# Second product's result in columns of 512 and 256, with w_out's conversion and the gate's weights placed later

## The chip, the core and the metric

One NeuronCore of a Trainium2 chip runs the whole program. The metric is the device time of one execution in microseconds (us). Engines are named as in the profile: PE (TensorE matmul), PEld (its weight loads), DVE (VectorE), ACT (ScalarE), POOL (GpSimd), SP (SyncE, whose queue issues most DMAs).

## What is computed

Three layers in a row. First an attention over 4 batches, 12 heads, 448 tokens, head size 64, with an RMS norm of q and k. Its output, 1792 tokens by 768, goes through a dense layer with ELU, and then through a mixture of 8 experts with a greedy assignment of tokens: every expert takes at most 224 tokens, in the order of all logits.

```python
scores = 1/8 * norm(q) @ norm(k).T ; attn = softmax(scores) ; x = attn @ v
h = x @ w_in                      # 768 -> 2048
x = elu(h) @ w_out                # 2048 -> 768      "the second product"
logits = x @ w_gate               # 768 -> 8; sorted, assigned greedily, 224 tokens an expert
out[tokens of e] = relu(x[tokens of e] @ w1[e]) @ w2[e]     # 768 -> 1024 -> 768
```

## The kernel before, in words

Every float32 matrix is split into two float16 parts (high and low), and a product is made of three float16 products (`THREE`, line 496), so a tile costs three matmuls.

The kernel first goes through 24 **pairs of heads** (6 a batch), 16 slots of a written schedule each (lines 737 to 757). A pair is scores (`ps`), softmax on DVE, ACT and POOL (`pe`, `sm`), transposes of the weights (`pta`, `ptb`) and the values (`po`); line 578 on ACT evicts a pair's values, once a pair, and so marks its end. Side work is spread over these slots by the table `spreads` (lines 728 to 733): w_in's conversion from float64 (`w_in_steps`), the hidden layer of the batch before (`hidden`: `ph`, then ELU in `elu_e`, `elu_g`, `gt`), **w_out's conversion** and its product with the gate's weights (`gate_products`, in slots 180 to 280), and the logits of batches 0 and 1 (`late_logits`, slots 295 to 400, `pl`). The logits are taken from the hidden layer directly, with Wg = w_out @ w_gate, which `gate_product` (line 619) makes in 16 pieces f, `pw` on PE and `wgt`/`Wg` on ACT and DVE.

One piece of w_out costs two DMA loads, six DVE instructions (lines 374, 377, 378, at 512 and 256 columns), ACT's lines 380 and 381, POOL's line 382, a store to DRAM and two DMA transposes on SP's queue. `load_gate` (line 597) loads and splits w_gate; `at(-30, load_gate)` puts it before the first scores.

The slots give the order of the program text; a scheduler then orders each engine's instructions, and each engine runs its own list strictly in order.

After the pairs come the hidden layer of the last batch, and the **second product** (`second`, line 804): for each of 14 blocks of 128 tokens, two column halves of DH = 384, 48 matmuls each (`py`), evicted by ACT and DVE to `xh` and stored to DRAM in `x2_d[0]` or `x2_d[1]`. For the last two batches all first halves are made before all second halves (lines 834 to 837). The routing (`Route`) runs in its gaps. Then each expert gathers its tokens' rows from `x2_d[0]` and `x2_d[1]` by POOL's indirect DMAs (`gather`, `xg`), PE transposes them (`pte`), ACT and DVE copy them to `xTe`. Expert 0 first does all products over the first half's KH = 3 chunks of 128 columns, then those of the second half; its inner tiles are `phe` and `phy`, the experts' outputs `pye`. Expert 0's weights are loaded during the routing.

```python
    spreads = [
        ...
        Spread(gate_products(), NG, 180, 280),
        Spread(chain_gens(late_logits(b) for b in range(LB)), 2 * LB * NF // LG, 295, 400),
    ]
    at(-47, load_gain)
    at(-30, load_gate)
```

Of the kernel before, what the change touches and what calls it, by code (L numbers as in the profile page):

```python
# [8 lines left out]
F16 = mybir.dt.float16  # L9
# [246 lines left out]
def kernel(  # L256
# [14 lines left out]
    nc = tc.nc  # L271
    PE, ACT, DVE, POOL = nc.tensor, nc.scalar, nc.vector, nc.gpsimd

    B, H, S, D = q.shape
# [7 lines left out]
    KC = DM // P  # L282
    NF = FF // P
    NF1 = F1 // P
    DH = DM // 2
    NJ = 3
    MAIN = NJ * P
    TAIL = S - MAIN
# [47 lines left out]
    g_d = [dram.tile([P, NF, 2, MAIN], F16, name=f"g_d{b}") for b in range(B)]  # L336

    gt_d = [dram.tile([P, NF, 2, 2 * TAIL], F16, name=f"gt_d{b}") for b in range(B // 2)]
    x2_d = [dram.tile([NCH * P, DM], F16, name=f"x2_d{i}") for i in range(2)]
    wo_d = dram.tile([P, NF, 2, DM], F16, name="wo_d")  # L340

    wuA = ctx.enter_context(tc.tile_pool(name="wuA", bufs=2))
# [254 lines left out]
    def load_gate():  # L597
        nc.sync.dma_start(wg32, w_gate.rearrange("(c p) e -> p c e", p=P))
        ACT.activation(wg16[:, :, 0:NE], wg32, AF.Copy, scale=-SW)
        DVE.scalar_tensor_tensor(wg16[:, :, NE:], wg32, -SW, wg16[:, :, 0:NE], op0=ALU.mult, op1=ALU.subtract)  # L600

    def gate_products():
        wts = None
        for f in range(NF):
            wo = gat.tile([P, 2, DM], F16, name="wo")
            yield from load_steps(wo[:, 0, :], wo[:, 1, :], w_out[f * P:(f + 1) * P, :])
            if f:
                gate_product(f - 1, wts)
                yield
            nc.sync.dma_start(wo_d[:, f], wo)  # L610
            wts = []
            for z in range(2):
                wts.append(gat.tile([P, KC, P], F16, name="wt", bufs=3))
                nc.sync.dma_start_transpose(wts[z], wo[:, z, :])
            yield
        gate_product(NF - 1, wts)
        yield

    def gate_product(f, wts):
# [14 lines left out]

    def logits(pool, tag, b, gs):

        pl = pool.tile([P, S], F32, tag=tag, name="pl")
        kk = key()
        for i, (g, f) in enumerate(gs):
            for z, (o, n) in enumerate(((0, WG), (WG, NE))):  # L640
                mm(pl[o:o + n], Wg[:, f, o:o + n], g[:, z, :], key=kk,
                   start=(i == 0), stop=(i == len(gs) - 1), skip_group_check=True)
        n = WG + NE
        for o, w, c in ((b * MAIN, MAIN, 0), (B * MAIN + b * TAIL, TAIL, MAIN)):
            a = acc[:, o:o + w]
            if gs[0][1] == 0:
                DVE.tensor_copy(a, pl[0:n, c:c + w])
            else:
                DVE.tensor_add(a, a, pl[0:n, c:c + w])

    LB = 2

    def late_logits(b):
        for f in range(0, NF, LG):
            gs = []
            for i in range(f, f + LG):
                gl = gat.tile([P, 2, S], F16, bufs=LG, name="gl")
                nc.sync.dma_start(gl[:, :, 0:MAIN], g_d[b][:, i])
                nc.sync.dma_start(gl[:, :, MAIN:S], gt_d[b // 2][:, i, :, b % 2 * TAIL:(b % 2 + 1) * TAIL])
                gs.append((gl, i))  # L660
            yield
            logits(psT, "pt", b, gs)
            yield

    def hidden(b, xT):

# [57 lines left out]
    def at(t, f, *a):  # L724
# [3 lines left out]
    spreads = [  # L728
        Spread(w_in_steps(0), KC, 40, 96),
        Spread(chain_gens(w_in_steps(i) for i in range(1, FF // WB)), KC * (FF // WB - 1), 96, 176),  # L730
        Spread(gate_products(), NG, 180, 280),
        Spread(chain_gens(late_logits(b) for b in range(LB)), 2 * LB * NF // LG, 295, 400),
    ]
    at(-47, load_gain)
    at(-30, load_gate)
    NSTEP = B * SEQ
    for b in range(B):
        xT = big.tile([P, KC, 2, S], F16, name="xT")
# [56 lines left out]

    gtp = []
    load_g(0)
    xo = rs_.enter_context(tc.tile_pool(name="xo", bufs=3))
    yp = [(psS, "ps")]

    def mmo(*x, **kw):
# [1 line left out]

    def second(rows, g, cols, i):

        o, n = i * DH, DH
        xh = xo.tile([P, 2, DH], F16, name="xh")
        py = yp[-1][0].tile([P, n], F32, tag=yp[-1][1], name="py")
        for f in range(NF):
            u, fu = divmod(f, NF // NU)  # L810
            for (a, z) in THREE:
                mmo(py, g_sb[g][:, f, z, cols], w_out_u[u][:, fu, a, o:o + n],
                    start=(f == 0 and a == 0 and z == 0), stop=(f == NF - 1 and z == 1))
                yield 0.165
        ACT.activation(xh[:, 0], py, AF.Copy, scale=-SX2 / (SG * SW))  # L815
        DVE.scalar_tensor_tensor(xh[:, 1], py, -SX2 / (SG * SW), xh[:, 0], op0=ALU.mult, op1=ALU.subtract)
        nc.sync.dma_start(x2_d[i][rows * P:(rows + 1) * P, :], xh.rearrange("p z d -> p (z d)"))
        yield 0.0
# [68 lines left out]
    rs_.close()  # L887
    psP.append(ctx.enter_context(tc.tile_pool(name="psP0", bufs=1, space=PSUM)))
    ex = ctx.enter_context(tc.tile_pool(name="ex", bufs=2))
    KH = KC // 2  # L890

    def pace_first(e, c):

# [14 lines left out]

    def gather(e):

        xT = [exg.tile([P, 2, KH, CAP], F16, name=f"xTe{i}") for i in range(2)]
        for i in range(2):
            for hh in range(2):
                xg = exg.tile([HD, 2, DH], F16, name="xg", bufs=4)
                POOL.indirect_dma_start(
                    out=xg.rearrange("p z d -> p (z d)"), out_offset=None, in_=x2_d[i],
                    in_offset=bass.IndirectOffsetOnAxis(ap=idx[:, 0, 2 * e + hh:2 * e + hh + 1], axis=0))
                pt = psX.tile([P, 2, KH, HD], F16, tag="pt", name="pte")
                for z in range(2):
                    for c in range(KH):  # L920
                        tr16(pt[:, z, c, :], xg[:, z, c * P:(c + 1) * P], HD)
                (DVE.tensor_copy if hh else ACT.copy)(xT[i][:, :, :, hh * HD:(hh + 1) * HD], pt)  # L922
        return xT
# [91 lines left out]
```

## Time and profile before

| | |
|---|---|
| median of 3 runs | 1150.81 us (1146.79 to 1153.8) |
| the profiled execution's own time | 1149.89 us |
| its span, first to last instruction | 1148.2 us |
| mean granted clock of PE | 0.968 |
| pairs of heads | to about 540 us |
| last hidden layer | about 540 to 620 us |
| second product and routing | about 620 to 883 us |
| experts | about 883 us to the end |

A page's or an answer's row gives busy time of an engine, mean duration of one instruction in ns, and the idle time before it with what ended it. "PEclk" is the share of full clock that PE was granted. Busy PE is not PE at its peak, since matmuls overlap: the distance from start to start tells what one costs.

### The profile page before, as it was taken

Reading aid. Unit: us, or ns where it says so; the run is one execution under the profiler, and the core shown is the slowest. Engines: PE = TensorE matmul, PEld = TensorE weight load, DVE = VectorE, ACT = ScalarE, POOL = GpSimd, SP = SyncE. Lnnn points to the kernel's source line nnn. Section 1 sums busy time; section 2 is a strip of 40 time slices with the busy share of each in tenths; the row PEclk is TensorE's granted clock in tenths of the full one; section 3 lists DMA queues with packets and bytes.
Section 4 is the critical chain, followed back from the end, with each engine's and each line's share of the span. In section 5 each row is a group of like instructions: output and inputs, shape, how many; then the busy total and the mean of one; then the engine's idle time right before and its main releaser. Section 6 shows DMA issues by size and latency. Waiting matters only on the chain.

```text
span 1148.2 us, 19348 instructions
## 1 busy us (share of the span) xinstructions
PE 1037.0 (90%) x7030; PEld 608.9 (53%) x7030; DVE 787.0 (69%) x1567; ACT 538.5 (47%) x1099; POOL 354.1 (31%) x462
## 2 busy tenths in 40 slices
PE   0687879897989989999999999999999799999997
PEld 0233434443544444444444545555546688888885
DVE  3798898999988775654334778887786556666620
ACT  2676677776867765554441111011112455555510
POOL 3677686657756542221001000000000412222100
PEclk9977889999999999999999999999999899999999
DMA  6355575559998736334922151131133778777710
GB/s 173 80 123 130 136 206 164 152 162 246 259 246 207 193 74 135 97 80 148 398 78 69 59 196 59 49 132 49 49 104 100 238 244 247 255 252 255 239 41 25
DMA packets 190319, 176.48 MB, mean 154 GB/s; under 512 B 114704, under 2 KB 161808, under 8 KB 189456
## 3 DMA queue, kind: packets, MB, share of 16 engines
q1 hardware_dynamic: 186064, 163.78, 49.7%
q0 software_dynamic: 3328, 11.01, 3.0%
q8 instruction: 55, 0.90, 0.3%
q10 hardware_dynamic: 832, 0.46, 0.1%
q14 instruction: 40, 0.33, 0.1%
HBM read 125.92 MB, written 31.98 MB: 138 GB/s over the span
## 4 chain that ended last, share of the span: by engine, by line
PE 51%; DVE 18%; DMA 11%; issue 10%; ACT 5%; POOL 3%; SPq 2%; POOLq 0%; DVEq 0%; ACTq 0%
PE py L324 18%; PE ph L324 11%; DMA st<-in_moe_w_dram 4%; PE pye L324 4%; PE po L324 4%; PE phe L324 3%; DVE sm L533 2%; PE ps L324 2%; PE rt_pc L324 2%; DVE cv L377 2%; PE pta L324 2%; DMA qn<-in_q_dram 2%; PE pl L324 1%; DVE cv L378 1%; DVE rt_C L127 1%
## 5 line engine op out<-in xcount | busy, mean ns | idle before, releaser
L324 PE MATMUL ph<-xT,w_in 128*128 128x448 f16 x1152 | 247.2, 359 | 7.8 <-DVE elu_g L685 4.8
L324 PE MATMUL py<-w_out,g 128*128 128x384 f16 x1152 | 203.8, 328 | 0.0
L324 PEld LDWEIGHTS <-w_in 128*128 128x128 f16 x1152 | 108.0, 99 | 125.4 <-issue 44.7
L545 POOL TENSOR_SCALAR pe<-pe,sm 128x448 f32<-128x448 f32 x168 | 127.0, 766 | 141.0 <-DVE sm L541 78.9
L351 DVE SCALAR_TENSOR_TENSOR w<-st,w 128x768 f16<-128x768 f32 (+1 forms) x112 | 119.4, 1073 | 72.1 <-ACT w L350 65.8
L324 PEld LDWEIGHTS <-g 128*128 128x128 f16 x1152 | 107.3, 98 | 81.4 <-issue 18.5
L350 ACT ACTIVATE w<-st 128x768 f16<-128x768 f32 (+1 forms) x112 | 103.8, 933 | 89.3 <-DMA st<-in_moe_w_dram 84.0
L324 PE MATMUL ps<-kT,qT 64*128 64x448 f16 (+1 forms) x576 | 94.3, 382 | 54.5 <-ACT pe L535 29.2
L535 ACT ACTIVATE pe<-ps,sm 128x448 f32<-128x448 f32 x168 | 105.7, 633 | 50.1 <-DVE sm L533 47.6
L324 PE MATMUL pye<-w,hT 128*112 128x512 f16 (+1 forms) x768 | 126.4, 326 | 0.0
L127 DVE TENSOR_SCALAR rt_C<-rt_row,rt_m 128x1792 f16<-128x1792 f32 x98 | 107.3, 1149 | 8.2 <-PE rt_pc L324 7.4
L533 DVE TENSOR_REDUCE sm<-ps 128x1 f32<-128x448 f32 x168 | 100.2, 614 | 17.8 <-PE ps L324 15.5
L324 PEld LDWEIGHTS <-w 128*128 128x128 f16 x1152 | 110.4, 99 | 3.3 <-DVE xTe L922 1.2
L324 PE MATMUL phe<-xTe,w 128*128 128x224 f16 x1080 | 109.2, 261 | 2.1 <-DVE xTe L922 1.1
L324 PEld LDWEIGHTS <-hT 128*112 128x112 f16 x768 | 91.6, 130 | 32.1
L815 ACT ACTIVATE xh<-py 128x384 f16<-128x384 f32 x28 | 13.7, 490 | 176.6 <-PE py L324 159.2
L324 PEld LDWEIGHTS <-qT 64*128 64x128 f16 (+1 forms) x576 | 27.5, 100 | 99.0 <-issue 65.9
L324 PE MATMUL pta<-id,pe 128*128 128x128 f32 x384 | 65.3, 293 | 12.7 <-POOL pe L545 4.7
L685 DVE SCALAR_TENSOR_TENSOR elu_g<-ph,elu_e 128x448 f32<-128x448 f32 x64 | 39.6, 618 | 48.0 <-ACT elu_e L683 47.7
L972 POOL DMA_INDIRECT out_dram<-yo,idx x16 | 18.5, 1155 | 173.9 <-DVE yo L971 172.3
L324 PEld LDWEIGHTS pta<-id,pe 128*128 128x128 f32 x384 | 46.1, 148 | 43.1 <-POOL pe L545 16.0
L201 POOL MEMSET rt_c<- 128x8 f16 x8 | 0.9, 123 | 210.1 <-DVE rt_c L207 206.0
(176 smaller groups left out, 1475.1 us busy)
## 6 DMA issues: line engine op xcount, KB each, us to landing
st<-in_moe_w_dram SPq DMA_DIRECT2D x48, 512.0 KB
st<-in_moe_w_dram SPq DMA_DIRECT2D x64, 384.0 KB
st<-in_moe_w_in_dram SPq DMA_DIRECT2D x24, 512.0 KB
g_d<-gt SPq DMA_DIRECT2D x64, 192.0 KB
g<-g_d SPq DMA_DIRECT2D x16, 768.0 KB
st<-in_moe_w_out_dram SPq DMA_DIRECT2D x16, 512.0 KB
gl<-g_d SPq DMA_DIRECT2D x32, 192.0 KB
wo_d<-wo SPq DMA_DIRECT2D x16, 384.0 KB
```

The source lines that it names most:

```text
L127: i = DVE.tensor_scalar(C.rearrange("p c t -> p (c t)"), row, m[:, s:s + 1], None, op0=ALU.is_le)
L324: i = PE_mm(o, l, r, **kw)
L350: ACT.activation(hi, st, AF.Copy, scale=SW)
L351: DVE.scalar_tensor_tensor(lo, st, SW, hi, op0=ALU.mult, op1=ALU.subtract)
L377: DVE.scalar_tensor_tensor(cv, st[:, :, 1], -0x40000000, cv, op0=ALU.bitwise_and, op1=ALU.bitwise_or)
L378: DVE.scalar_tensor_tensor(cv, st[:, :, 0], 29, cv, op0=ALU.logical_shift_right, op1=ALU.bitwise_or)
L533: i = DVE.tensor_reduce(out=st[:, 0, u:u + 1], in_=ps[u], axis=AX.X, op=ALU.max, negate=True)
L535: ACT.activation(p[:, u, :], ps[u], AF.Exp, bias=st[:, 0, u:u + 1], accum_out=st[:, 1, u:u + 1])
L545: POOL.tensor_scalar(p[:, u, :], p[:, u, :], st[:, 2, u:u + 1], 1.0, op0=ALU.mult, op1=ALU.mult)
L685: DVE.scalar_tensor_tensor(gf, ph, -SG / SH, e, op0=ALU.mult, op1=ALU.min)
L815: ACT.activation(xh[:, 0], py, AF.Copy, scale=-SX2 / (SG * SW))
L972: st = POOL.indirect_dma_start(out=out, out_offset=bass.IndirectOffsetOnAxis(ap=idx[:, 1, 2 * e + hh:2 * e + hh + 1], axis=0), in_=yo, in_ ...
```

## The change

1. The second product's columns are divided 512 and 256 (`PARTS`) instead of 384 and 384, and with them `x2_d`, `xh`, `xg` and `xTe`; expert 0's first round has KH = 4 of 6 chunks. `xg` has two tags with two buffers each, `xh` two buffers instead of three.
2. `gate_products` moves from slots 180 to 280 to slots 240 to 368; `late_logits` goes over f first, then over the batches, in slots 285 to 400.
3. `load_gate` moves from slot -30 to slot 100 of the program text.

```diff
-    DH = DM // 2
+    PARTS = ((0, 512), (512, DM - 512))
...
-    x2_d = [dram.tile([NCH * P, DM], F16, name=f"x2_d{i}") for i in range(2)]
+    x2_d = [dram.tile([NCH * P, 2 * n], F16, name=f"x2_d{i}") for i, (_, n) in enumerate(PARTS)]
...
-    def late_logits(b):
+    def late_logits():
         for f in range(0, NF, LG):
-            gs = []
-            for i in range(f, f + LG):
...
+            for b in range(LB):
+                gs = []
+                for i in range(f, f + LG):
...
-        Spread(gate_products(), NG, 180, 280),
-        Spread(chain_gens(late_logits(b) for b in range(LB)), 2 * LB * NF // LG, 295, 400),
+        Spread(gate_products(), NG, 240, 368),
+        Spread(late_logits(), 2 * LB * NF // LG, 285, 400),
     ]
     at(-47, load_gain)
-    at(-30, load_gate)
+    at(100, load_gate)
...
-    xo = rs_.enter_context(tc.tile_pool(name="xo", bufs=3))
+    xo = rs_.enter_context(tc.tile_pool(name="xo", bufs=2))
...
-        o, n = i * DH, DH
-        xh = xo.tile([P, 2, DH], F16, name="xh")
+        o, n = PARTS[i]
+        xh = xo.tile([P, 2, n], F16, name="xh")
...
-                yield 0.165
+                yield 0.165 * n / 384
...
-    KH = KC // 2
+    KH = PARTS[0][1] // P
...
-        xT = [exg.tile([P, 2, KH, CAP], F16, name=f"xTe{i}") for i in range(2)]
+        xT = [exg.tile([P, 2, n // P, CAP], F16, name=f"xTe{i}") for i, (_, n) in enumerate(PARTS)]
         for i in range(2):
             for hh in range(2):
-                xg = exg.tile([HD, 2, DH], F16, name="xg", bufs=4)
+                n = PARTS[i][1]
+                xg = exg.tile([HD, 2, n], F16, tag=f"xg{i}", name="xg", bufs=2)
```

**Where the instructions go.** Counted in PE's list between the ends of pairs (the 14 `po` matmuls of one pair to those of the next):

| intervals between pairs' ends | before | changed |
|---|---|---|
| 11th to 15th (four) | `pw` 108, `ph` 215 | `pw` 0, `ph` 180 |
| 15th to 23rd (eight) | `pw` 84 (first three), `ph` 348, `pl` 72 | `pw` 192 (24 each), `ph` 414, `pl` 72 |
| 23rd to 24th (one) | `pw` 0, `ph` 46, `pl` 8 | `pw` 0, `ph` 30, `pl` 8 |
| after the last pair | `ph` 273 | `ph` 258 |

DVE's list, right behind the end of the 12th pair, before:

```order
L579 SCALAR_TENSOR_TENSOR xT<-po,xT 128x448
L560 COPY PT<-ptb 128x3x128
L378 SCALAR_TENSOR_TENSOR cv<-st,cv 128x256
L628 TENSOR_TENSOR wgt<-wgt,pw 128x8
L374 TENSOR_SCALAR cv<-st 128x256
L377 SCALAR_TENSOR_TENSOR cv<-st,cv 128x512
L540 TENSOR_SCALAR sm<-sm 128x2
L533 TENSOR_REDUCE sm<-ps 128x1 x2
L629 CAST Wg<-wgt 128x8
L630 CAST Wg<-wgt 128x8
```

and in the changed kernel at the same place (its lines are some six higher):

```order
L580 SCALAR_TENSOR_TENSOR xT<-po,xT 128x448
L561 COPY PT<-ptb 128x3x128
L534 TENSOR_REDUCE sm<-ps 128x1 x2
L561 COPY PT<-ptb 128x3x128
L541 TENSOR_SCALAR sm<-sm 128x2
L542 RECIPROCAL sm<-sm 128x2
L534 TENSOR_REDUCE sm<-ps 128x1 x2
L691 SCALAR_TENSOR_TENSOR elu_g<-ph,elu_e 128x448
```

The softmax's reductions (`sm<-ps`) stand there without w_out's steps (`cv`, `wgt`, `Wg`) ahead of them. Those now stand in the late pairs; DVE's list of the changed kernel behind the end of the 20th pair, where before has none of them:

```order
L580 SCALAR_TENSOR_TENSOR xT<-po,xT 128x448
L561 COPY PT<-ptb 128x3x128
L534 TENSOR_REDUCE sm<-ps 128x1
L375 TENSOR_SCALAR cv<-st 128x512
L378 SCALAR_TENSOR_TENSOR cv<-st,cv 128x512
L541 TENSOR_SCALAR sm<-sm 128x1
L379 SCALAR_TENSOR_TENSOR cv<-st,cv 128x512
L542 RECIPROCAL sm<-sm 128x1
L691 SCALAR_TENSOR_TENSOR elu_g<-ph,elu_e 128x448
```

A reduction that stood directly behind the matmuls' results now has up to two conversions in front of it.

POOL's list at the first gathers, before (x_d_82 is `x2_d[0]`, x_d_83 is `x2_d[1]`; a row is two gathers, one for each half of an expert's tokens):

```order
L915 DMA xg<-x_d_82,idx 112x768 x2
L915 DMA xg<-x_d_83,idx 112x768 x2
L915 DMA xg<-x_d_82,idx 112x768 x2
L915 DMA xg<-x_d_83,idx 112x768 x2
L915 DMA xg<-x_d_82,idx 112x768 x2
```

and in the changed kernel:

```order
L922 DMA xg<-x_d_82,idx 112x1024 x4
L922 DMA xg<-x_d_83,idx 112x512 x4
L922 DMA xg<-x_d_82,idx 112x1024 x2
L922 DMA xg<-x_d_83,idx 112x512 x2
L922 DMA xg<-x_d_82,idx 112x1024 x2
```

Expert 1's rows of the first part are now fetched before expert 0's rows of the second. On PE, before runs the 72 products of expert 0's first round, then 18 `pte` (12 of expert 0's second part, 6 of expert 1), then the second round. The changed kernel runs 70 of its 96, four `pte` of the second part, two more products, four `pte`, the other 24, 16 `pte` of expert 1, then the second round of 48. The gate's weights come earlier than their new slot: on DVE line 600's instruction stands behind the last of the first pair's preparation, before the first reduction of scores, where it stood ahead of the second sum of squares.

## Rows read from the trace of the kernel before

**Rows 1.** The page: the span.
```profile
span 1148.2 us, 19348 instructions
```

**Rows 2.** Windows: length; busy PE, PEld, DVE, ACT, POOL (count); PEclk, DMA share, GB/s.
```profile
252.00:354.00 102.00, 89.08 (x577) 44.13 (x574) 96.33 (x223) 74.25 (x183) 68.36 (x80) 0.95 0.99 251
...
411.00:517.00 106.00, 102.31 (x626) 49.26 (x623) 66.39 (x161) 61.90 (x149) 30.69 (x46) 1.00 0.40 93
```

**Rows 3.** Line 578, the pairs' ends: 11th to 17th, then 18th to 24th.
```profile
L578 ACT ACTIVATE xT<-po x7: 521/527/536, 254.7 to 407.2; 128x448 f16<-128x448 f32 x7
L578 ACT ACTIVATE xT<-po x7: 543/543/543, 421.6 to 538.6; 128x448 f16<-128x448 f32 x7
```

**Rows 4.** Windows, DVE alone, instructions on tile cv (w_out's conversion).
```profile
250.00:411.00 161.00, 48.35 (x89) 0.97 0.91 226
```

**Rows 5.** The same for tile wgt (the sums behind the gate's product).
```profile
250.00:411.00 161.00, 16.61 (x60) 0.97 0.91 226
```

**Rows 6.** The chain of work that ended last: start, us, what.
```profile
324.82 3.38 PE po L324 x14
...
354.58 3.16 PE po L324 x14
...
517.85 3.16 PE po L324 x14
...
535.38 3.16 PE po L324 x14
538.54 1.62 PE pl L324 x15
...
549.57 3.52 PE ph L324 x18
...
1003.84 15.60 PE pye L324 x96
```

**Rows 7.** Line 688 on DVE in 252 to 411 us, then in 411 to 535 us.
```profile
L688 DVE TENSOR_TENSOR gt<-elu_g,gt 128x448 f16<-128x448 f32 x19 | 14.4, 759 | 1.6 <-ACT gt L687 1.6
L688 DVE TENSOR_TENSOR gt<-elu_g,gt 128x448 f16<-128x448 f32 x15 | 9.7, 649 | 3.9 <-ACT gt L687 3.7
```

**Rows 8.** Timeline of the start: start, us, engine, line, [idle before <- releaser].
```profile
11.90 2.07 POOL L454 TENSOR_TENSOR qn<-qn,gain 128x896 f32<-128x896 f32 x1 [8.40 <-DMA vn<-in_v_dram]
...
12.04 1.99 DVE L600 SCALAR_TENSOR_TENSOR wg<-wg,wg 128x48 f16<-128x48 f32 x1 [0.38 <-ACT wg L599]
13.96 1.07 DVE L452 TENSOR_REDUCE ss<-sq 128x14 f32<-128x896 f32 x1
...
15.53 0.21 POOL L465 TENSOR_SCALAR ss<-ss 128x28 f32<-128x28 f32 x1 [1.56 <-ACT ln L459]
```

**Rows 9.** Timeline from the second product to expert 0.
```profile
875.71 7.63 PE L324 MATMUL py<-w_out,g 128*128 128x384 f16 x46
...
884.56 0.34 SPq L817 DMA_DIRECT2D x_d<-xh  x1
...
888.47 3.61 PE L324 MATMUL phy<-xTe,w 128*128 128x224 f16 x36
...
890.84 1.82 POOL L915 DMA_INDIRECT xg<-x_d,idx  x1 [11.35 <-issue]
...
896.32 0.47 PE L324 MATMUL pte<-id,xg 112*128 112x112 f16 x6 [4.24 <-DMA xg<-x_d,idx]
...
897.88 0.74 PE L324 MATMUL pte<-id,xg 112*128 112x112 f16 x6 [1.09 <-DMA xg<-x_d,idx]
```

**Rows 10.** PE alone, a little later: expert 0's second round and the start of its outputs.
```profile
900.78 4.67 PE L324 MATMUL phe<-xTe,w 128*128 128x224 f16 x31
...
912.53 15.76 PE L324 MATMUL pye<-w,hT 128*112 128x512 f16 x96
```

**Rows 11.** Windows there, columns as in rows 2.
```profile
895.00:900.00 5.00, 1.21 (x12) 0.82 (x12) 1.34 (x2) 1.46 (x2) 3.54 (x4) 0.71 0.94 281
900.00:905.00 5.00, 4.76 (x35) 4.18 (x36) 1.17 (x3) 2.22 (x4) 0.93 (x1) 0.61 0.61 173
```

More of the change, by code (lines that the diff above doesn't have):

```diff
@@ L600, in load_gate @@
         DVE.scalar_tensor_tensor(wg16[:, :, NE:], wg32, -SW, wg16[:, :, 0:NE], op0=ALU.mult, op1=ALU.subtract)
+    ready = []
     def gate_products():
-        wts = None
         for f in range(NF):
@@ L608, in gate_products @@
                 gate_product(f - 1, wts)
+                ready.append(f - 1)
                 yield
@@ L616, in gate_products @@
         gate_product(NF - 1, wts)
+        ready.append(NF - 1)
         yield
@@ L635, in logits @@
     def logits(pool, tag, b, gs):
+        assert gs[-1][1] in ready
         pl = pool.tile([P, S], F32, tag=tag, name="pl")
@@ L651 @@
     LB = 2
-    def late_logits(b):
+    def late_logits():
         for f in range(0, NF, LG):
-            gs = []
-            for i in range(f, f + LG):
[L657 to L663, printed above, removed]
+            for b in range(LB):
+                gs = []
+                for i in range(f, f + LG):
+                    gl = gat.tile([P, 2, S], F16, bufs=LG, name="gl")
+                    nc.sync.dma_start(gl[:, :, 0:MAIN], g_d[b][:, i])
+                    nc.sync.dma_start(gl[:, :, MAIN:S], gt_d[b // 2][:, i, :, b % 2 * TAIL:(b % 2 + 1) * TAIL])
+                    gs.append((gl, i))
+                yield
+                logits(psT, "pt", b, gs)
+                yield
     def hidden(b, xT):
@@ L917, in gather @@
                     in_offset=bass.IndirectOffsetOnAxis(ap=idx[:, 0, 2 * e + hh:2 * e + hh + 1], axis=0))
-                pt = psX.tile([P, 2, KH, HD], F16, tag="pt", name="pte")
+                pt = psX.tile([P, 2, n // P, HD], F16, tag="pt", name="pte")
                 for z in range(2):
-                    for c in range(KH):
+                    for c in range(n // P):
                         tr16(pt[:, z, c, :], xg[:, z, c * P:(c + 1) * P], HD)
```

## The prediction, made before the changed kernel ran

> **What bounds the kernel now.** I read the mean clock and the busy shares in 40 slices first, then windows by stage, then the chain of work that ended last, then the timelines of the three places that the change touches. The span is 1148.2 us [rows 1]; the execution's own time is 1149.9, so 1.7 us lie around it, and it stands 0.9 us under the median of 1150.8. All sums below are made against 1149.9.
>
> The pairs of heads have two regimes, and the reader should see both in [rows 2]. From 252 to 354 us, while w_out is converted, DVE is busy 96.33 of 102 us (94%), the DMA engines 0.99, PE 89 of 102 at a granted clock of 0.95: PE waits for a softmax that stands in DVE's list behind conversions. From 411 to 517 us, with w_out done, PE is busy 102.31 of 106 us and DVE only 66.39 (63%), DMA 0.40: here PE is the bound. The ends of the pairs give what this costs [rows 3]: seven pairs from 254.7 to 421.6 us, 23.8 us each with w_out; six from 421.6 to 538.6 us, 19.5 us each without. The change moves w_out's work from the first regime towards the second. After the pairs, PE has work without a break; that stretch is only touched where it hands over to the experts, where PE stands idle [rows 9].
>
> **The change, part by part.**
>
> *The gate's weights.* At the start DVE's line 600 takes 1.99 us, from 12.04, between the gain and the second sum of squares at 13.96; POOL then begins the Newton step at 15.53, although its own work ended at 11.90 + 2.07 = 13.97 [rows 8]. In the changed list line 600 stands behind the first pair's preparation. The sum of squares can come 1.9 us earlier, and POOL can start at 13.97: 1.56 us saved, limited by POOL. What hides line 600 at its new place is DVE's wait for the first scores; without that cover its 1.99 us come back. So between 0 and 2.0 us saved; I take **-1.5**, what POOL's row allows.
>
> *w_out, early pairs.* Four intervals, from the end of the 11th pair to the end of the 15th, lose all w_out work: no `pw` is left in them in PE's list. They have 45 `ph` each, like the six late pairs (45.5 each) that took 19.5 us. Those also had 13 logits matmuls; 15 of them took 1.62 us [rows 6], so 1.4 us go off: 18.1. The early pairs still have the preparation of later heads on ACT, DVE and POOL beside them. Low end 18.1, high end 23.8 (as if w_out cost nothing there); I take 18.5, near the low end because DVE loses most of its load: 74 us.
>
> *w_out, late pairs.* Eight intervals, to the end of the 23rd pair, now carry two of the 16 pieces each. One piece costs DVE 48.35 us for 89 instructions, six a piece, so 3.26 us [rows 4], and 16.61 us for 60, four a piece, so 1.11 us [rows 5]: 4.4 us together, 8.8 a pair. DVE's load without it is 66.39 us in 106 us of 19.5 us pairs, 12.2 a pair [rows 2, 3]. The sum of 21.0, at the 94% that DVE reached in the first regime, is 22.4 us a pair. PE's own bound: 19.5, plus 6.25 more `ph` at 3.52/18 = 0.196 [rows 6], 1.2, plus some 0.5 for a more even share of scores, plus 24 `pw`. These have no price of their own in the rows; they lie between 0 and the logits' 0.108 us each, nearer 0 as they have 16 or 8 columns against 448, so 0.6. That makes 21.8 us. Two engines within 3% of each other, and a DMA queue that was full with w_out, do not both run at their limit. The nearest row for such a stretch is before's own with w_out, 23.8 us at 2.3 pieces a pair: the changed pairs have 0.3 pieces fewer (1.3 us of DVE) but 4 more `ph` (0.7) and nine logits matmuls (0.9). I take **23.8**, 190.4 us for eight. The ends are 21.8 (PE alone) and 29.8, the costliest single pair of before with w_out, 324.82 to 354.58 [rows 6].
>
> Here a rule of the Trainium skill can be weighed. Line 688 on DVE reads two tiles in SBUF and took 759 ns while POOL was busy 67% of the time, 649 ns where POOL was busy 29% [rows 2, 7]. The Trainium skill, SBUF — State Buffer, section "Who interferes with whom", says that a DVE instruction with two SBUF inputs contends with a GpSimd instruction that reads SBUF, one blocking the other entirely; these rows agree with it. By that rule the conversions would cost less late: if half of line 688's 14% is gained, 0.3 us a piece, 4.8 us over 16 pieces, and the forecast would be about 1134. I keep to the measured 4.4 us, since w_out's POOL step moves along and no row shows the conversions late.
>
> *The last pair and the tail.* The last interval took 17.5 us, 517.85 to 535.38 [rows 6]; with 30 `ph` in place of 46 it loses 16 x 0.196 = 3.1: 14.4 us. After the last pair 258 `ph` are left in place of 273: 15 x 0.196 = **-2.9**, since PE is without a break there. The three parts give 74 + 190.4 + 14.4 = 278.8 us where before has 538.6 - 254.7 = 283.9: **-5.1**.
>
> *Logits and SP's queue.* `late_logits` has the same 16 steps; its loads now stand among w_out's loads on SP's queue, one behind the other. I cost the order itself at nothing; hidden layers and logits cover it, and the third rival prices it if that cover is gone. The stores of w_out to DRAM end well before they are read back behind the last pair.
>
> *512 and 256 columns.* The number of matmuls and weight loads stays. Expert outputs have just these widths: 48 matmuls of 512 and 48 of 256 in 15.60 us, 0.325 a couple [rows 6]; 46 `py` of 384 took 7.63, two of them 0.332 [rows 9]. Nothing, then, between 0 and a few us less. The evictions keep their number and bytes and lie beside PE. With two `xh` buffers a store must have landed two parts later: it took 6.3 us, 884.56 to 890.84 [rows 9], and two parts of 256 columns take 2 x 48 x 0.108 = 10.4 us. If that failed, ACT would wait, with one more accumulator free for PE.
>
> *The hand-over.* Before, the 72 products of the first round end at 888.47 + 3.61 = 892.1; the last store lands at 890.84; the second part's rows reach PE at 896.32 and 897.88; the second round starts at 900.78, the outputs at 912.53 [rows 9, 10]. In the changed list PE runs 70 of 96 products (0.0985 each, to about 892), then meets the second part's transposes and waits to about 896, and for their second half to about 897.9; behind it stand 24 products (900.3), 16 transposes of expert 1, whose rows are no longer fetched behind the last store, 26 products, 8 transposes, 22 products (906.3), 25 products of expert 1 and 16 transposes: outputs at about 909.6, with six more products done. That is 3.5 us. Against it stands the clock: the granted clock was 0.71 from 895 to 900 and 0.61 from 900 to 905 [rows 11], so PE was on the lower of its two levels (1.2 instead of 2.4 GHz) for some 6.8 us after its idle stretch: the missing 0.29 and 0.39 of 5 us each, by a half, and 31 products took 4.67 us [rows 10] in place of 3.05. If the clock falls again, with more products in that stretch, up to 3.4 us are given back; the larger gathers of expert 1 beside the last store could cost 1 us more. Between -3.5 and +1; I take **-2.0**. It passes to the end: from 912.53 to the outputs at 1003.84 [rows 6, 10] lie three experts of 30.4 us, just PE's own work of 144 products and 15.6 us of outputs with their transposes.
>
> Sum: -1.5 - 5.1 - 2.9 - 2.0 = -11.5; 1149.9 - 11.5 = **1138.4 us**.
>
> **The rivals.**
> 1. *PE alone sets the late pairs* (21.8 us each). For it: DVE is 37% idle there. Against it: 21.8 and 22.4 are too close. 8 x 2.0 = 16 us less: 1122.4.
> 2. *The load costs late what it freed early.* Late pairs at 25.4 us, what six of the early ones took (254.7 to 407.2 [rows 3]). For it: reductions stand behind conversions on DVE again, and PE has less slack to lose. 8 x 1.6 = 12.8 more: 1151.2, no change to be measured.
> 3. *Slower: SP's queue becomes the pace of the late pairs.* A logits load waits there for a `gl` buffer that PE frees; w_out's loads and transposes queue behind it, then DVE's conversions, then the reductions behind them. At 27 us a pair, between 23.8 and the worst 29.8: 8 x 3.2 = 25.6 more, 1164. It decides from 26.1 us a pair on. Against it: w_out's tiles and `gl` have buffers of their own, and the DMA share there is 0.40 [rows 2].
> 4. *The change does not do what it says*: the scheduler already hoists the gate's load, so that the start and the hand-over give nothing: 1141.9.
>
> **How the numbers follow.** Forecast 0.47 (late pairs of 22.8 to 25 us: 1130 to 1148), rival 1 0.19, rival 2 0.18, rival 3 0.11, rival 4 0.05. A measurement of this kernel can tell about 0.5%, 5.8 us, from no change: faster means under 1145.0, late pairs under 24.6. Faster: 0.40 of the forecast, rival 1, most of rival 4: 0.63. Same: 0.25. Slower: rival 3 and a little more, 0.12. The range of 1122 to 1152 takes in the forecast, rivals 2 and 4 and the upper half of rival 1; it leaves out rival 3 and the rest of rival 1.
>
> **What would show it.** Pair ends about 18.5 us apart from the 11th to the 15th and 23.8 from there to the 23rd; DVE busy near 90% in the latter, PE at full clock in both. POOL's Newton step at about 14 us. Expert outputs 2 to 3.5 us sooner behind the last `py`. I am wrong if the early pairs stay above 20 us, if the late ones leave 22.8 to 25, or if SP's waits show logits loads ahead of w_out's.

## The result, and the profile after

The changed kernel takes **1137.24 us** (median of 4 runs, 1132.28 to 1139.79) beside 1151.24 for the kernel before on the same chip: a ratio of 0.9877, 95% interval 0.9832 to 0.9923. The forecast was 1138.4 and "faster". The profiled execution took 1139.79 us, the slowest of the four; its span answers to [rows 1]. All differences in the table below are of the two profiled spans: 1148.2 to 1137.9, 10.3 us less, where the medians are 14.0 us apart.

```profile
span 1137.9 us, 19336 instructions
```

Both traces are cut at the same events; the middle columns come from the timelines of the two kernels. A mark is the start of its instruction; `plt` is the first matmul of the routing.

| stretch | before, us | after, us | difference | forecast |
|---|---|---|---|---|
| start to the 11th pair's end | 254.7 | 253.9 | -0.8 | -1.5 |
| 11th to 15th pair end | 105.0 | 75.9 | | 74 |
| 15th to 23rd pair end | 161.4 | 187.4 | | 190.4 |
| 23rd to 24th pair end | 17.5 | 14.1 | -6.5 for the three | 14.4; -5.1 |
| 24th pair end to the first `plt` (routing) | 79.8 | 77.0 | -2.8 | -2.9 |
| first `plt` to the last `py` (second product) | 264.6 | 262.0 | -2.6 | 0 |
| last `py` to the end of the span | 265.2 | 267.6 | +2.4 | -2.0 |

The pairs' ends, as in [rows 3] (the line is now 579), first the 11th to the 17th, then the 18th to the 24th:

```profile
L579 ACT ACTIVATE xT<-po x7: 536/544/545, 253.9 to 377.3; 128x448 f16<-128x448 f32 x7
L579 ACT ACTIVATE xT<-po x7: 534/537/544, 403.4 to 531.3; 128x448 f16<-128x448 f32 x7
```

Windows of the early and the late pairs, columns as in [rows 2]:

```profile
253.90:329.80 75.90, 75.45 (x438) 37.06 (x438) 56.52 (x114) 52.65 (x123) 39.46 (x51) 1.00 0.42 106
329.80:517.20 187.40, 176.80 (x1178) 85.60 (x1177) 161.12 (x399) 129.42 (x323) 93.16 (x120) 0.98 0.83 205
```

PE is now busy 99% of the early pairs and 94% of the late ones, DVE 86% of the late ones. In the kernel before, the stretch that held w_out was this:

```profile
254.70:421.60 166.90, 144.27 (x965) 72.80 (x964) 148.22 (x353) 117.83 (x293) 103.92 (x127) 0.97 0.85 212
```

PE 86%, DVE 89%. What PE waited for there stands in the groups of PE's instructions by line and tile (behind the bar: busy us, mean ns; then us idle just before them and what ended it). Before, 254.7 to 421.6 us:

```profile
L324 PE MATMUL ps<-kT,qT 64*128 64x448 f16 (+1 forms) x167 | 26.6, 370 | 10.3 <-ACT pe L535 10.3
```

After, 329.8 to 517.2 us:

```profile
L325 PE MATMUL ps<-kT,qT 64*128 64x448 f16 (+1 forms) x198 | 31.0, 355 | 0.7 <-ACT pe L536 0.6
```

This is where the time came from. Scores wait for a buffer that the exponentials `pe` free; those wait for DVE's reductions, which stood behind conversions. Before, that cost PE 10.3 us in seven pairs; in the eight late pairs of the changed kernel, with two pieces of w_out a pair instead of 2.3 and more hidden-layer products beside them, 0.7 us. ACT still waits for the reductions there, and longer than before. Before and after, the same stretches:

```profile
L535 ACT ACTIVATE pe<-ps,sm 128x448 f32<-128x448 f32 x49 | 30.8, 632 | 7.6 <-DVE sm L533 7.3
```

```profile
L536 ACT ACTIVATE pe<-ps,sm 128x448 f32<-128x448 f32 x59 | 37.4, 636 | 23.7 <-DVE sm L534 23.2
```

So ACT waits for the reductions more than before, and PE less for ACT: PE has other work meanwhile. No run separates the fewer conversions a pair from the additional products. From the 11th to the 24th pair's end, before and then after, PE's idle time falls from 22.6 to 12.3 us, and 3.9 us more of PE's work (products taken out of the tail among it) lie in that stretch, which leaves the 6.5 us:

```profile
254.70:538.60 283.90, 261.27 (x1673) 129.49 (x1673) 215.41 (x516) 183.04 (x447) 131.61 (x172) 0.98 0.68 167
```

```profile
253.90:531.30 277.40, 265.12 (x1692) 129.65 (x1694) 221.13 (x521) 184.77 (x449) 132.62 (x170) 0.99 0.69 172
```

The conversions of w_out (tile `cv`, DVE alone, as in [rows 4]) and the sums (tile `wgt`, as in [rows 5]) now lie in the late pairs:

```profile
329.80:517.20 187.40, 50.80 (x87) 0.98 0.83 205
```

```profile
329.80:517.20 187.40, 14.48 (x64) 0.98 0.83 205
```

The start, with the rows that answer to [rows 8]. The Newton step begins at 14.29 instead of 15.53, the first scores at 23.9 instead of 25.2 and the first pair ends 1.4 us sooner; at the 11th pair's end 0.8 us of it is left.

```profile
11.82 1.08 DVE L453 TENSOR_REDUCE ss<-sq 128x14 f32<-128x896 f32 x1
...
12.13 2.07 POOL L455 TENSOR_TENSOR qn<-qn,gain 128x896 f32<-128x896 f32 x1 [8.62 <-DMA vt<-in_v_dram]
...
14.29 0.21 POOL L466 TENSOR_SCALAR ss<-ss 128x28 f32<-128x28 f32 x1
...
20.54 0.21 DVE L601 SCALAR_TENSOR_TENSOR wg<-wg,wg 128x48 f16<-128x48 f32 x1
```

The hand-over, answering to [rows 9] and [rows 10]:

```profile
869.10 3.50 DVE L352 SCALAR_TENSOR_TENSOR w<-st,w 128x1024 f16<-128x1024 f32 x3 [2.87 <-DMA x_d<-xh]
...
870.36 2.60 SPq L363 DMA_DIRECT2D st<-in_moe_w_dram  x3
...
872.51 0.42 DVE L822 SCALAR_TENSOR_TENSOR xh<-py,xh 128x256 f16<-128x256 f32 x1
...
873.05 0.38 SPq L823 DMA_DIRECT2D x_d<-xh  x1
...
878.13 2.27 PE L325 MATMUL phy<-xTe,w 128*128 128x224 f16 x22
...
881.59 1.68 POOL L922 DMA_INDIRECT xg<-x_d,idx  x1 [8.08 <-issue]
...
885.95 0.55 PE L325 MATMUL pte<-id,xg 112*128 112x112 f16 x4 [5.54 <-DMA xg<-x_d,idx]
...
901.44 15.76 PE L325 MATMUL pye<-w,hT 128*112 128x512 f16 x96
```

The last `py` starts at 870.3, but DVE's half of its eviction stands behind three conversions of expert 1's weights; the store goes out at 873.05, and the gather that needs it starts only 8.5 us later (6.3 before). PE has done its 70 products by 880.4, waits 5.5 us and then runs below full clock, as in [rows 11]:

```profile
885.00:890.00 5.00, 2.98 (x20) 2.24 (x21) 1.46 (x3) 3.06 (x4) 1.87 (x2) 0.53 0.64 211
890.00:895.00 5.00, 5.00 (x51) 4.61 (x50) 2.42 (x4) 1.94 (x3) 1.40 (x2) 0.79 0.77 245
```

### The profile page after: what moved, and what is told of

Its sections match the earlier page's. It is cut to its first block, busy times and chain, and to the rows that moved or that the text cites. A ratio compares the mean times of both kernels' runs of the same rounds, so it can differ in the third digit from the quotient of the medians.

```text
span 1137.9 us, 19336 instructions
## 1 busy us (share of the span) xinstructions
PE 1032.5 (91%) x7030; PEld 606.1 (53%) x7030; DVE 788.4 (69%) x1567; ACT 538.9 (47%) x1099; POOL 353.5 (31%) x462
## 4 chain that ended last, share of the span: by engine, by line
PE 50%; DVE 18%; DMA 11%; issue 10%; ACT 5%; POOL 3%; SPq 2%; POOLq 0%; DVEq 0%; ACTq 0%
PE py L325 17%; PE ph L325 13%; DMA st<-in_moe_w_dram 6%; PE po L325 4%; PE pye L325 4%; PE ps L325 3%; DVE sm L534 2%; PE rt_pc L325 2%; DVE w L352 2%; PE pta L325 2%; DVE cv L378 2%; DVE cv L375 2%; ACT w L351 1%; DVE rt_C L127 1%; DMA qn<-in_q_dram 1%
## 5 line engine op out<-in xcount | busy, mean ns | idle before, releaser
L325 PE MATMUL py<-w_out,g 128*128 128x256 f16 (+1 forms) x1152 | 203.1, 326 | 0.0
L546 POOL TENSOR_SCALAR pe<-pe,sm 128x448 f32<-128x448 f32 x168 | 129.4, 780 | 125.3 <-DVE sm L542 49.5
L325 PE MATMUL ps<-kT,qT 64*128 64x448 f16 (+1 forms) x576 | 95.2, 381 | 47.6 <-DMA qT<-h 23.9
L821 ACT ACTIVATE xh<-py 128x512 f16<-128x512 f32 (+1 forms) x28 | 13.7, 490 | 171.7 <-PE py L325 158.5
L325 PE MATMUL pta<-id,pe 128*128 128x128 f32 x384 | 65.3, 294 | 14.4 <-POOL pe L546 5.7
L922 POOL DMA_INDIRECT xg<-x_d,idx x32 | 37.6, 1175 | 94.4 <-DVE idx L252 53.8
```

What stands on the lines that cost most here:

```text
L325: i = PE_mm(o, l, r, **kw)
L546: POOL.tensor_scalar(p[:, u, :], p[:, u, :], st[:, 2, u:u + 1], 1.0, op0=ALU.mult, op1=ALU.mult)
L922: POOL.indirect_dma_start(out=xg.rearrange("p z d -> p (z d)"), out_offset=None, in_=x2_d[i], in_offset=bass.IndirectOffsetOnAxis(ap=idx[: ...
```

## The experiments

Marks of every run in us, from its one profiled execution (pairs: 11th to 24th pair end; product: first `plt` to last `py`; outputs: last `py` to first `pye`; end: last `py` to the end of the span), and the ratio to the kernel before on the same chip with its 95% interval.

| run | pairs | product | outputs | end | median | ratio |
|---|---|---|---|---|---|---|
| before | 283.9 | 264.6 | 29.5 | 265.2 | 1151.24 | 1 |
| after | 277.4 | 262.0 | 31.1 | 267.6 | 1137.24 | 0.9877 (0.9832 to 0.9923) |
| e1_parts | 286.5 | 262.0 | 28.5 | 266.5 | 1152.95 | 1.0001 (0.9976 to 1.0025) |
| e2_wout | 276.5 | 262.9 | 28.2 | 267.7 | 1140.5 | 0.9902 (0.987 to 0.9934) |
| e3_gate | 286.2 | 264.6 | 28.8 | 265.1 | 1150.55 | 0.9986 (0.9962 to 1.0011) |
| e4_wout_gate | 276.7 | 264.5 | 29.2 | 269.8 | 1139.34 | 0.9889 (0.9857 to 0.992) |
| e5_store_act | 278.5 | 262.0 | 30.8 | 267.3 | 1139.08 | 0.9871 (0.9837 to 0.9906) |
| e6_hold | 277.0 | 263.8 | 26.4 | 266.7 | 1138.22 | 0.9867 (0.9835 to 0.9899) |
| e7_dve2_after | 287.0 | 263.7 | 28.6 | 266.6 | 1148.04 | 0.9961 (0.9937 to 0.9985) |
| e8_dve2_before | 299.3 | 263.0 | 29.0 | 265.3 | 1164.62 | 1.0104 (1.0062 to 1.0146) |
| e9_batch | 278.7 | 262.1 | 29.8 | 267.0 | 1137.98 | 0.9861 (0.9815 to 0.9908) |
| e10_hold_stx | 276.0 | 262.0 | 22.5 | 265.9 | 1136.56 | 0.9855 (0.9808 to 0.9901) |
| e11_wide | 276.1 | 264.0 | 28.6 | 267.1 | 1138.2 | 0.987 (0.9824 to 0.9916) |
| e12_xg4 | 279.2 | 263.7 | 24.6 | 257.4 | 1130.51 | 0.9799 (0.9777 to 0.9821) |

**The three parts, one at a time.** e1 is the kernel before with the new columns alone, e2 with w_out's steps and the order of the late logits alone, e3 with the gate's weights alone; e4 is the changed kernel with

```
-    PARTS = ((0, 512), (512, DM - 512))
+    PARTS = ((0, DM // 2), (DM // 2, DM // 2))
```

> The kernel before with the columns 512 and 256 alone (w_out's steps, the late logits and the gate's weights stay as they were). Theory A, the parts add: the second product, from the first plt to the last py, takes 262 us where before took 264.6, the stretch from the last py to the first pye 31 us where before took 29.5, the pair ends of the 11th to the 24th pair keep 283.9 us; 1151 us +- 1.5 in all, no change. Rival B, the 2.6 us of the second product and the 1.6 us lost behind it come from w_out's later steps (other places of the weights' loads and conversions): 264.6 us and 29.5 us as before, again 1151. Rival C, the columns alone cost something where w_out is as before: over 1154.

> The kernel before with w_out's steps from 240 to 368 and the late logits taken four blocks at a time for both batches; columns in halves, the gate's weights early. Theory A: 11th to 24th pair end 277.4 us instead of 283.9, 24th pair end to plt 77.0 instead of 79.8, the second product 264.6 and last py to first pye 29.5 as before: 1142 us (-9.3). Rival B: the second product 262 us and last py to first pye 31 also here: 1141, told apart by the marks. Rival C, w_out's move needs the gate's weights out of the start to pay: 1146 or more.

> The kernel before with the gate's weights loaded at step 100 instead of -30, nothing else. Theory A: first ps 1.3 us sooner, of which 0.8 us is left at the 11th pair end and at the end of the span: 1150.4 us. Rival B: the 1.3 us stays to the end: 1149.8; its pair ends tell: all 1.3 to 1.5 us sooner. Rival C: nothing is left by the 7th pair, because the loads of w_in and of the heads set the pace there: 1151.

> The changed kernel with the columns in halves again (384 and 384, three xh buffers, four xg). Theory A: the second product 264.6 us and last py to first pye 29.5, the rest as in the changed kernel: its span is 2.6 - 1.6 = 1.0 us longer at the first pye, and some 0.2 us at the end, as the columns' gain and loss nearly cancel: 1137.5 to 1138.5 us. Rival B, the columns bring most of what came (over 4 us): 1141 or more. Rival C, the columns cost: under 1136.

w_out's move is the change: e2 alone gives 11.2 us, where the medians of before and after are 14.0 apart. e1 gives nothing that can be measured, e3 1.2 us with an interval that holds no change. e4, without the columns, lies between its theories A and B at 1139.34; its interval covers the changed kernel's ratio, so the columns' share of the total can't be told from nothing. Programs with the same w_out steps differ by some 3 us between the 11th and the 24th pair: 283.9, 286.5 and 286.2 with the old ones, 276.0 to 279.2 with the new ones (after, e2, e4, e5, e6, e10, e12). By their means, 285.5 and 277.3, the move is worth 8.2 us there, and 2.8 us in the tail: 11.0, which is e2's gain.

Of the second product's 2.6 us, theory A gave all to the columns, and e1 seems to agree with 262.0. It falls all the same: e2, with halves, needs 262.9, e6 and e12, with the new columns, 263.8 and 263.7. What parts them is the clock just behind the first `plt`. Before, then after, 10 us from there:

```profile
618.40:628.40 10.00, 9.39 (x64) 6.15 (x64) 6.00 (x16) 1.17 (x2) 0.00 (x0) 0.83 0.33 115
```

```profile
608.30:618.30 10.00, 9.43 (x65) 5.41 (x66) 7.77 (x18) 1.17 (x2) 0.00 (x0) 1.00 0.35 120
```

The granted clock in that window is 0.83 in before, e3, e4, e6, e7, e11 and e12 and 1.00 in after, e1, e2, e5, e8, e9 and e10. Halves: 264.6 with the fall, 262.9 without; 512 and 256: 263.8 and 262.0. So 1.7 us are the clock, which falls with either width, and 0.8 to 0.9 us the columns. Why it falls in some of these executions and not in others stays open.

In the hand-over the columns bring the second part's rows later. With 512 and 256 DVE's half of the last eviction stands behind conversions in the changed kernel, e1, e7, e9 and e11 alike, and the last store goes out 2.7 us behind the last `py`; with halves (before, e2, e3, e4, e8) it goes out after 1.5 us. The gather that needs the store starts 10.3 to 11.3 us behind the last `py` in the first group and 7.8 to 8.2 in the second, and the rows reach PE after 14.9 to 15.6 and 12.8 to 13.4 us. That the outputs come as late as 31.1 us is not the columns: e1, with its rows at 15.2 us, has 28.5. Its list of PE has 87 products ahead of the transposes that wait for these rows, as in e7 and e11 (28.6 both), where the changed kernel's has 70: the scheduler orders them anew in every program. Seventeen products are 1.7 us of work that lies inside the wait instead of behind it. PE in e1:

```profile
886.83 6.43 PE L325 MATMUL phe<-xTe,w 128*128 128x224 f16 x48 [2.14 <-DVE xTe L928]
893.10 3.90 PE L325 MATMUL phy<-xTe,w 128*128 128x224 f16 x39
898.88 0.37 PE L325 MATMUL pte<-id,xg 112*128 112x112 f16 x4 [1.88 <-DMA xg<-x_d,idx]
```

The clock adds to it: in the 5 us from the arrival of the rows it was 0.68 in e1 and 0.50 in the changed kernel, 0.9 us of difference.

```profile
898.90:903.90 5.00, 3.60 (x32) 3.06 (x33) 2.13 (x3) 2.26 (x4) 2.04 (x3) 0.68 0.60 201
```

```profile
885.90:890.90 5.00, 3.88 (x24) 2.97 (x25) 2.36 (x4) 2.83 (x4) 1.87 (x2) 0.50 0.57 187
```

**Which engine holds the late pairs.** e7 and e8 do DVE's third conversion step twice for w_out, in the changed kernel and in the one before; e9 does three short steps once for two rows of blocks (a row of blocks is one of w_out's 16 pieces); e11 spreads w_out wider.

```
+            if twice:
+                DVE.scalar_tensor_tensor(cv, st[:, :, 0], 29, cv, op0=ALU.logical_shift_right, op1=ALU.bitwise_or)
```

```
-        DVE.tensor_copy(Wg[:, f, 0:NE], t)
...
+        if f % 2:
+            t, fs = two[0], slice(f - 1, f + 1)
+            DVE.tensor_copy(Wg[:, fs, 0:NE], t)
...
```

```
-        Spread(gate_products(), NG, 240, 368),
-        Spread(late_logits(), 2 * LB * NF // LG, 285, 400),
+        Spread(gate_products(), NG, 210, 372),
+        Spread(late_logits(), 2 * LB * NF // LG, 290, 400),
```

> The changed kernel with DVE's third step of each conversion of w_out done twice (the second time it changes nothing): some 1.1 us more of DVE for each of 16 rows of blocks, two of them in each late pair. Theory P, the late pairs are bound by PE (176.8 of 187.4 us busy in this kernel) and DVE has room: 15th to 23rd pair end up to 5 us longer, 1138 to 1142 us. Theory V, the prediction's, DVE bounds them: 2.3 us a pair, 15 to 18 us longer, 1152 to 1155 us.

> The same doubled step in the kernel before, where the 16 rows of blocks lie in the 11th to the 18th pair. Theory V for the early pairs, DVE is the bound there (99.3 of 105.0 us busy): 1.1 us for each row of blocks, 14 to 18 us more, 1165 to 1169 us. Rival: the DMA engines (0.99 busy there) are the bound, DVE merely follows: under 6 us more, under 1157 us.

> The changed kernel with DVE's three short steps behind a gate product (lines 633 to 635, 0.37, 0.16 and 0.33 us each) done once for two rows of blocks instead of for each: some 7 us of DVE less in the eight late pairs, PE's work the same. The doubled step cost 11.3 us of the late pairs for some 18 us of DVE, a slope of 0.64. Theory M, both DVE and PE hold the late pairs: the same slope, 15th to 23rd pair end 183 us instead of 187.4, 1133 to 1135 us. Theory P, PE alone holds them in the changed kernel (DVE came in only when it was doubled): 186 to 188 us, 1138 us. Theory V: 180 us, 1131 us.

> The changed kernel with w_out's steps from 210 to 372 and the late logits from 290 to 400. 16 rows of blocks in 10.1 pairs instead of 8, 1.6 a pair instead of 2. Theory M: DVE 1.8 us a pair less in the late pairs, at a slope of 0.64 9 us less from the 15th to the 23rd pair end; the two pairs before take three rows of blocks, 13 us of DVE, where DVE was busy 74% and PE 99%: 4 us more there. 1132 to 1135 us. Theory P, PE holds both: no change, 1138 us. Rival: the early pairs lose more than the late ones gain, over 1141 us.

In e7 the 15th to the 23rd pair end take 198.7 us, 11.3 more, between the two theories. The conversions cost 69.97 us of DVE there, 19.2 more than in the changed kernel, so 0.6 us for each us of them; DVE's whole busy time grows by 14.8 us, since its other instructions take less. And PE's wait for the softmax is back, which shows that DVE's conversions can make it (329 to 518 us):

```profile
L325 PE MATMUL ps<-kT,qT 64*128 64x448 f16 (+1 forms) x192 | 31.6, 364 | 9.6 <-ACT pe L538 9.5
```

In e8 the same steps cost 14.9 us from the 11th to the 18th pair end, 12.3 us in the median, under theory V's 14; the DMA engines as the only bound there, under 6 us, are ruled out. DVE is busy 166.14 us there in place of 148.22, 17.9 more and 91% of the stretch, so it was most of the bound in the early pairs, and not all. The late pairs in e7, then the early ones in e8:

```profile
328.20:526.90 198.70, 182.16 (x1187) 87.88 (x1184) 175.92 (x429) 130.91 (x324) 98.45 (x122) 0.97 0.80 196
```

```profile
254.60:436.40 181.80, 151.16 (x963) 75.17 (x963) 166.14 (x379) 120.26 (x294) 110.70 (x128) 0.92 0.81 197
```

e9 took 6.7 us off DVE's short steps (`wgt` 7.80 instead of 14.48 us) and the late pairs took 188.6 us, no less: a miss for theories M and V, but a weak test, since DVE's whole busy time fell only from 161.12 to 158.86 us. e11 is the stronger one: DVE has 18.2 us less in the late pairs, yet they take 186.9 us instead of 187.4, with PE busy 96% of them (3.3 us more of its work lies there). All pairs take 276.1 us instead of 277.4, within what programs with the same steps differ by. The late pairs in e9, then in e11:

```profile
330.10:518.70 188.60, 177.01 (x1178) 85.73 (x1177) 158.86 (x375) 129.32 (x322) 92.59 (x120) 0.98 0.84 204
```

```profile
331.10:518.00 186.90, 180.11 (x1180) 88.55 (x1180) 142.94 (x370) 125.30 (x311) 88.00 (x115) 0.98 0.76 182
```

So DVE is close behind PE in the changed kernel but no longer decides: more of it costs, less of it gives nothing that can be measured. That PE's own work sets the pace there follows from its 94%; no run changed that work.

**The hand-over.** e5 issues the last store on another queue, e6 orders expert 1's first conversions behind the last eviction, e10 adds six load buffers for the later experts, e12 then doubles the buffers of gathered rows.

```
-        nc.sync.dma_start(x2_d[i][rows * P:(rows + 1) * P, :], xh.rearrange("p z d -> p (z d)"))
+        (nc.scalar if i and rows == B * NJ - 1 else nc.sync).dma_start(x2_d[i][rows * P:(rows + 1) * P, :], xh.rearrange("p z d -> p (z d)"))
```

```
+        for i, o in zip((x, y), behind):
+            tc.add_manual_dep(i.ins, o.ins.name, NOSYNC, reason="behind the last eviction")
```

```
+    stx = ctx.enter_context(tc.tile_pool(name="stx", bufs=6))
...
-                xg = exg.tile([HD, 2, n], F16, tag=f"xg{i}", name="xg", bufs=2)
+                xg = exg.tile([HD, 2, n], F16, tag=f"xg{i}", name="xg", bufs=4)
```

> The changed kernel, the last store of the second product's rows issued by ACT's queue instead of SP's, nothing else. Theory D, the hand-over waits for this store because it stands on SP's queue behind three loads of 512 KB (issued from 870.36 us on, the store at 873.05, the gather it releases at 881.59): on a queue of its own it lands 2.5 to 4 us after its issue instead of 8.5, the second part's transposes come 4 us sooner, last py to first pye 27 us instead of 31, the end 1133 to 1136 us if it passes to the end. Rival E, the transfers share the same engines whatever queue issues them, and 1.5 MB are under way: landing 7 to 9 us after issue as now, 1137 us. Rival F, the late eviction is what matters (DVE's half of it stands at 872.51, behind three conversions of weights): at most 1 us gained.

> The changed kernel with expert 1's first conversions ordered behind the last eviction on ACT and on DVE, nothing else; SP then issues the loads that those conversions make room for behind the store too. Theory D: eviction done 1.2 us after the last py instead of 2.6, store landed 3 to 4 us after its issue, PE's wait behind the first 70 products (5.5 us) gone, last py to first pye 25 to 27 us; 1132 to 1135 us if it passes to the end. Rival G, expert 1's weights come 3 us later and PE waits for them there: first pye 25 to 27 us after the last py, the second expert's outputs no sooner than now, 1137 us.

> The kernel with expert 1's first conversions held behind the last eviction, and from expert 1's fourth block on six buffers of their own for the weights' loads in place of the three. Theory D2: the 4.7 us won at the first pye were lost in expert 2 because ACT stood 3.3 us at a conversion whose load had not landed, with the copy of expert 2's rows queued behind it; with more loads under way ACT does not wait, the gain reaches the end: 1133 to 1134.5 us, third outputs at 957 instead of 961. Rival H, the loads are limited by the transfer rate (0.88 of the DMA engines busy there): the wait stays, 1138 us. Rival I, the new buffers stand where the second product's data lay, so the first loads start later and PE waits for expert 1's weights: over 1139 us.

> The kernel of the experiment with six load buffers (which held the weights' conversions behind the last eviction too), with four buffers instead of two for the gathered rows of each part, nothing else. There the first pye came 22.5 us after the last py instead of 31.1, and 8.2 us of that went again in expert 1 and 2: 5.7 us of PE waiting for expert 2's second rows, whose gathers are issued only when expert 1's have left their buffers, and 2.5 us of a lower granted clock behind that wait. Theory J, with the gathers an expert ahead the wait does not arise: last py to the end of the span 258 to 260 us instead of 265.8, 1129 to 1131 us. Rival K, the gathers are issued sooner but land late, since the loads take the DMA engines (0.93 busy there): the wait moves to another place, 265 us, 1136 us. Rival L, more gathers ahead of expert 0's second part on POOL's queue delay the hand-over itself: first pye 25 us or more after the last py, over 1137 us.

e5: the store went out on ACT's queue at 874.31 and the gather started at 882.07, 7.8 us later. The queue is not the cause, and theory D falls as it was put; rival E's 7 to 9 us came. The Trainium skill, DMA: Bandwidth & Descriptors, section "Issuing engines are not separate DMA queues", says that transfers run on the same 16 engines whatever engine started them; e5 agrees.

e6 won 4.7 us to the first `pye` and kept 0.9 of it to the end; the third outputs came at 961.2 instead of 961.5. Its store still landed late, 7.2 us after its issue and not 3 to 4. PE waited in expert 2 for ACT, and ACT for the loads of the weights. PE, then ACT, in e6:

```profile
950.42 0.53 PE L325 MATMUL pte<-id,xg 112*128 112x112 f16 x4 [2.99 <-ACT xTe L936]
```

```profile
948.73 0.84 ACT L352 ACTIVATE w<-st 128x768 f16<-128x768 f32 x1 [3.29 <-DMA st<-in_moe_w_dram]
949.48 1.32 ACT L936 COPY xTe<-pte 128x896 f16<-128x896 f16 x2
```

e10 won 8.6 us to the first `pye`, kept 1.7 of it to the end, and missed its forecast (1136.56 for 1133 to 1134.5). Its new buffers keep SP's weight loads away from the hand-over: no load goes out from 861.74 to 869.28 us. The store, issued at 867.30, had landed by 870.05, 2.75 us later, where 7.2 to 8.5 us passed in e6, e5 and the changed kernel with loads of 512 KB under way. SP's queue in e10:

```profile
861.74 5.88 SPq L829 DMA_DIRECT2D x_d<-xh  x2
869.28 14.88 SPq L366 DMA_DIRECT2D st<-in_moe_w_dram  x12
```

The gain again went, to expert 2's gathers, which stood on POOL's queue until their buffers came free. POOL, then PE, in e10:

```profile
904.70 0.94 POOL L930 DMA_INDIRECT xg<-x_d,idx  x1 [2.52 <-PE pte L325]
905.94 4.85 POOL L930 DMA_INDIRECT xg<-x_d,idx  x1 [0.30 <-issue]
911.10 0.96 POOL L987 DMA_INDIRECT out_dram<-yo,idx  x1 [0.31 <-issue]
912.36 1.00 POOL L930 DMA_INDIRECT xg<-x_d,idx  x1 [0.30 <-PE pte L325]
```

```profile
917.97 0.93 PE L325 MATMUL pte<-id,xg 112*128 112x112 f16 x8 [5.72 <-DMA xg<-x_d,idx]
918.70 9.56 PE L325 MATMUL phe<-xTe,w 128*128 128x224 f16 x72
```

72 products that take 7.06 us at full clock (in e12) took 9.56: 5.7 + 2.5 us were gone at this place. With four buffers (e12) the wait and the fall are absent, and PE is busy all of the first 51.1 us of outputs:

```profile
895.50:946.60 51.10, 51.10 (x420) 42.80 (x418) 35.44 (x43) 31.71 (x43) 12.85 (x10) 1.00 0.87 287
```

Last `py` to the end takes 257.4 us instead of 267.6, a little less than theory J's 258 to 260, and e12 runs in **1130.51 us**, faster than both kernels; its interval (0.9777 to 0.9821) ends below the changed kernel's 0.9832. It holds the edits of e6 and e10 too; the four buffers without them were not run.

## Why the prediction was right, and where it was not

- **Start, -1.5.** 1.4 us sooner at the first pair's end, as worked out, but 0.8 left at the 11th; e3 gives 1.2 in the median, not told apart from nothing. The limit by POOL was right, "saved" to the end was not.
- **Early pairs, 18.5 us each.** 19.0. The low end was the right side: PE 99% busy. Nine of w_out's 96 `cv` steps still lie there, though no `pw` does.
- **Late pairs, 23.8 each.** 23.4, in the forecast's band of 22.8 to 25, so the times of rivals 1 to 3 are out; SP's queue waited 3.7 us in all before logits loads there, too little for rival 3. Rival 4's mechanism is out, since line 601 now runs at 20.54, but its outcome, no gain from start and hand-over together, is what came. PE's own work was put at 21.8 and is 176.80/8 = 22.1 (DVE's 22.4 should have been 21.0/0.94 = 22.3); a row of blocks cost DVE 6 x 50.80/87 + 4 x 14.48/64 = 4.4 us, as taken. That the two engines would not both run at their limit holds. But DVE "near 90%" as the nearer bound is wrong: it is 86%, PE 94%, and by e11 and e7 these pairs are PE's until DVE gets more. That is rival 1's mechanism, at 23.4 us instead of its 21.8: PE still idles 1.3 us a pair.

```profile
SPq L664 <- PE pl L325: 3.7, 4, 2.0
```

- **Three stretches and the tail, -5.1 and -2.9.** -6.5 and -2.8.
- **Columns, 0.** Some -0.9 us by the table; the other 1.7 us there are the clock.
- **Hand-over, -2.0.** This step failed: +2.4. The rows of the second part were taken to reach PE when they did before, 13.3 us behind the last `py`; they came after 15.6, since the eviction stood behind conversions with the new columns (e6, where it does not: 13.2) and the store among the weights' loads (e10). From there to the outputs the sum had 13.3 us (896.3 to 909.6); 15.5 passed, at a clock of 0.53 and 0.79. That fall was priced, up to 3.4 us, but taken in only by half. "It passes to the end" was wrong too: e6 and e10 won 4.7 and 8.6 us at the first `pye` and gave 3.8 and 6.9 of it back at later waits. The stretch from there to the end, read as "just PE's own work", held waits: 235.7 us before, 236.5 in the changed kernel, 232.8 in e12.
- **The rule on the shared port.** What the prediction drew from it, conversions that become cheaper late (forecast 1134), did not come: a `cv` step took 50.80/87 = 584 ns late, and 45.90/87 = 528 ns in before's stretch of 254.7 to 421.6 us, although POOL was busy 50% of the one and 62% of the other. The sum rightly did not use it.
- **The total.** 1138.4 is 1.2 us above the median of 1137.24, but part of that is luck. The missed terms, -1.4 and -2.6 against +4.4, nearly cancel; and the sum of -11.5, between the 10.3 of the spans and the 14.0 of the medians, was taken from an execution 1.35 us under before's median of 1151.24.

What stays open: why the clock falls where it does in the hand-over and behind the first `plt`, and why the stretch behind the last `py` is 265.1 to 266.5 us in the four programs with w_out's old steps and 266.6 to 269.8 in the changed kernel and the others with the new ones, except e10 and e12.

## What to carry to other kernels

When side work stalls the bound engine in one stretch, first add up the bound engine's own work in all stretches that could take it: here PE was busy 144 of 167 us where the side work lay, and after the move 252 of the 263 us of the pairs that the move touched, which leaves little more to win by moving. A gain at a hand-over is real only if every in-order queue behind it (conversions waiting for loads, gathers waiting for buffers) is early too; follow it to the last instruction before counting it. A short store that someone waits for wants no bulk loads under way beside it; here 2.75 us passed without them and 7.2 to 8.5 with them, on either queue.

## What the runs showed of the hardware that I had not expected

DVE's line 600 took 1.99 us in [rows 8], nearly all of it beside a POOL instruction with two inputs; the same instruction took 0.21 us at its new place, with no POOL instruction beside it. Line 694 (two inputs in SBUF, 128x448) shows the same by instruction: 33 instructions with nothing on POOL beside them have a mean of 620 ns, 8 that mostly met line 383 (POOL's subtraction, two inputs) 1053 ns, and 15 that mostly met line 546 (one input) 701 ns. By stretch, early and late pairs of the changed kernel:

```profile
L694 DVE TENSOR_TENSOR gt<-elu_g,gt 128x448 f16<-128x448 f32 x10 | 6.7, 672 | 3.0 <-ACT gt L693 2.9
L694 DVE TENSOR_TENSOR gt<-elu_g,gt 128x448 f16<-128x448 f32 x24 | 18.2, 758 | 4.5 <-ACT gt L693 4.3
```

POOL is busy 52% of the one and 50% of the other. So POOL's busy share, by which I compared [rows 7], is the wrong measure; which instructions meet decides. The Trainium skill, SBUF — State Buffer, section "Who interferes with whom", says that a DVE instruction with two SBUF inputs contends with a GpSimd instruction that reads SBUF; the 1053 and 701 ns agree. The extra 1.8 us of line 600 look like such a meeting; no run moved the one without the other.
